# Loading four rows of w_down per partition at the very start of a decode block, with the unused matmuls of the tail laid out anew

## The chip, the cores and the metric

The kernel runs on one core of one Trainium2 chip. Its engines work side by side: TensorE (PE in the profile; PEld is its loading of weights), VectorE (DVE), ScalarE (ACT), GpSimd (POOL) and SyncE (SP). Here SP issues nearly all the transfers from the chip's memory; the transfers themselves run on 16 DMA engines. The metric is the time of one execution in microseconds (us). Lower is better. A profile shows one execution from the first to the last instruction, the span; the execution's own time is a little longer.

## The reference

One decode step of a transformer block for a single token: attention over a cache of 65,536 positions, then a gated feed-forward layer.

```
B, Sq, D = 1, 1, 1024;  Hq, Hkv, Sk, Dh = 32, 4, 65536, 128;  F = 3584      (bf16)

q = layernorm(x) @ wq                                  # 1024 x 4096
scores = q . k_cache * Dh**-0.5;  p = softmax(scores)  # 8 query heads share one k/v head
h = x + (p . v_cache) @ wo                             # 4096 x 1024
n = layernorm(h)
out = h + (gelu(n @ w_gate) * (n @ w_up)) @ w_down     # 1024 x 3584 twice, 3584 x 1024
```

Every weight and every cache entry is used once: 173 MB are read, nearly all of it the two caches.

## The kernel before, in words

The kernel is written by hand in program order. A small class, `Flow` (lines 17 to 105), records operations with the names of what each reads and writes, works out which waits between engines are needed, and `issue()` then sends them to the engines. Each engine does its own list in order and waits on semaphores. Everything from the first layer norm to the gated product is one such list, issued inside a section that the tile framework leaves alone (`tc.tile_critical`, line 587). At the start of a section SP executes a no-op that raises a semaphore, and the other engines wait for it; at its end SP waits for all engines. Line 95 is where `issue()` calls an operation, so most rows of the profile carry L95.

All transfers of weights and caches go through SP's one queue, in this order: w_q in two halves into slots 0 and 1 of a ring of four slots, then for each of 8 half-heads two K loads (slots 2 and 3) and one V load (slots 0 and 1), then wo, w_gate (7168 KB), w_up (7168 KB) and w_down. A load into a slot waits until the engines have finished with what was there. The small x goes through ACT's queue.

In the loop, DVE transposes K, PE makes the scores, ACT the exponentials, and PE multiplies by V. After the loop the attention output is normalised on DVE, and multiplied by wo. `ffn_in` (line 534) issues the load of w_gate or w_up, does 64 matmuls (eight input rows per partition, eight blocks each) and two DVE transposes. The product of gelu(gate) and up goes into `actz`, in columns padded with zeros so that a 32-wide window picks the row of the output that a matmul adds to.

w_down has 28 rows per partition, each 2 KB. The first 16 (`FA`) go to slot 0 in one load of 4096 KB, eight (`FB - FZ`) to slot 1 in one of 2048 KB, and the last four (`FZ`) to a buffer of their own, `w_end`, in two loads of three rows and one row (768 and 256 KB, line 592). The first of these two is issued at the end of the section, the second only once all engines have ended it. The output is summed in two banks of PSUM, `d_ps` and `d_odd`. The residual h is put there ahead, by eight small matmuls at line 568, while up's weights are on their way.

`down` (line 598) does one row of w_down: eight matmuls of 32 columns by 128, four of them side by side in the array. `parts` lists the two large loads with their semaphores. In a second section (line 610) PE waits for each in turn and does its rows; after that section it waits for the two loads of `w_end`. `stay_busy(n)` does n matmuls of 128 x 512 into a bank that nobody reads. Such matmuls compute nothing; in the kernel before there are four ahead of the wait for the 16 rows and four ahead of the wait for the eight. At the end DVE and ACT cast the two banks (lines 622 and 623) and SP sends the result out.

Of the kernel before, what the change touches and what calls it, by code (L numbers as in the profile page):

```python
# [11 lines left out]
BF16 = mybir.dt.bfloat16  # L12
# [4 lines left out]
class Flow:  # L17
# [13 lines left out]
    def op(self, e, call, r=(), w=(), after=(), wait=(), inc=None, dma=False, rows=None, **kw):  # L31
        i = len(self.ops)
        deps = {}

        def need(j, hard):
            o = self.ops[j]
            if o["e"] == e and not dma and not o["dma"] and (e == "pe" or not hard):
                return
            deps[j] = True

        for k in r:
            if k in self.writer:
                need(self.writer[k], True)
        for k in tuple(w) + tuple(after):
            if k in self.writer:
                need(self.writer[k], True)
            for j in self.readers.get(k, ()):
                need(j, False)
        if e == "pool":
            if self.rows[0] != rows and self.rows[1] is not None and not self.ops[self.rows[1]]["inc"]:  # L50
                deps[self.rows[1]] = True
            self.rows = rows, i
        last = {}
        for j in deps:
            o = self.ops[j]
            k = j if o["dma"] else o["e"]
            last[k] = max(last.get(k, j), j)
        deps = last.values()
        for k in r:
            self.readers.setdefault(k, []).append(i)  # L60
        for k in w:
            self.writer[k] = i
            self.readers[k] = []
        self.ops.append(dict(e=e, call=call, kw=kw, deps=sorted(deps), wait=wait, inc=inc, dma=dma))
# [44 lines left out]
def kernel(  # L109
# [13 lines left out]
    nc = tc.nc  # L123
    P = 128
    D = A_x.shape[-1]
# [4 lines left out]
    F = B_w_gate.shape[1]  # L130
    DC = D // P
# [14 lines left out]
    NB = 512  # L146
# [5 lines left out]
    eps = 1e-5  # L152
    assert Dh == P and rep * NS == SQ and NT % (CH * NH) == 0 and D % NB == 0 and F % NB == 0 and C4 == 4
    assert CPH == 4 and NH == 2

    FZ = 4
    w_end = nc.alloc_sbuf_tensor("w_end", [P, FZ, D], BF16)
# [3 lines left out]
    def sb(name, shape, dtype=F32):  # L161
        return const.tile(shape, dtype, name=name)
# [3 lines left out]
    qs = sb("qs", [P, 4, NS, P + 1], BF16)  # L166
    sc = sb("sc", [P, CPH, NN, rep, NS])
    pt = sb("pt", [P, CPH, NN, rep, NS], BF16)
    bank = [psum.tile([P, NB], F32, name="bank%d" % i) for i in range(8)]
    kt_bytes = ktb[:].rearrange("p c s w -> p (c s w)")  # L170

    def over(offset, shape, dtype=F32):

        n = 1
        for x in shape:
            n *= x
        if dtype == F32:
            v = kt_bytes[:, offset // 4:offset // 4 + n]
        else:
            v = kt_bytes[:, offset // 4:offset // 4 + n // 2].bitcast(BF16)  # L180
        if len(shape) == 2:
            v = v.rearrange("p (a b) -> p a b", a=shape[0])
        return v

    def slot(i, n=1):
        return ring[:, i * CW:(i + n) * CW]

    f = Flow(nc, tc)
    op = f.op
# [45 lines left out]
    def select(key, out, op_, fill, base, pattern, mult, rows=None):  # L235
# [14 lines left out]
       in_=ident_f[:].rearrange("p (q m) -> p q m", q=4).unsqueeze(2).to_broadcast([P, 4, NI, SQ]))  # L250
# [7 lines left out]
    sel16 = sb("sel16", [P, 16])  # L258
# [40 lines left out]
    def wide_rows(banks, bkeys, rows_z, zkey, ci, blocks, wkeys, first, last):  # L299

        for t, w in enumerate(blocks):
            q = t % 4
            op("pe", "matmul", r=[zkey] + wkeys, w=[bkeys[t // 4]], out=banks[t // 4][32 * q:32 * q + 32, :], lhsT=rows_z[:, ci, :], rhs=w,
               start=first, stop=last, tile_position=(0, 32 * q))

    def rows_to_columns(banks, bkeys, key, order="p n -> p n", **sizes):

        w = [ps.shape[-1] for ps in banks]
        r = over(28672, [sum(w)])
        o = 0  # L310
        for ps, n, bk in zip(banks, w, bkeys):
            src = ps.rearrange(order, **sizes)
            op("dve", "transpose", r=[bk], w=[key], out=r[:, o:o + n].rearrange("p (e j) -> p e j", j=32) if sizes else r[:, o:o + n], in_=src)
            o += n
        return r[:, 0:o:32]
# [10 lines left out]
    for q in range(4):  # L326
        op("pe", "matmul", r=["q_bf"] + ["esel"], w=["B5"], out=qsel_ps[:, :, q, :], lhsT=esel[:, q, :], rhs=q_bf[:],
           start=True, stop=True)
# [162 lines left out]
    for dq in range(OQ):  # L491
        op("pe", "matmul", r=["o_sb", "osel"], w=["B4"], out=o2_ps, lhsT=osel[:, dq, :], rhs=o_sb[:, dq * Hq:(dq + 1) * Hq],
           start=(dq == 0), stop=(dq == OQ - 1))
# [7 lines left out]

    FA = CW // D
    FB = FC - FA
    at_ps = bank[6][:]
    wv = slot(2, 2).rearrange("p (c n) -> p c n", c=Hq)
    f.dma("sp", wv, A_wo.rearrange("(p c) n -> p c n", p=P), w=["R2", "R3"], wait=done, sem=r_sem[2])
    for c in range(Hq):
        for s in range(DS):
            q = 2 * (c % 2) + s
            op("pe", "matmul", r=["o2z", "R2", "R3"], w=["B6"], out=at_ps[32 * q:32 * q + 32, :], lhsT=o2z[:, c, :],  # L510
               rhs=wv[:, c, :].rearrange("k (p s c) -> k s p c", s=DS, c=C4)[:, s], start=(c < 2), stop=(c >= Hq - 2), tile_position=(0, 32 * q))
# [12 lines left out]
    assert DC * F <= 2 * CW  # L524
    FW = [32 * FA, 32 * FB]

    def f_blocks(w_row):

        blocks = []
        for o, n in zip((0, P * FA), FW):  # L530
            blocks += [w_row[:, o + q * n:o + (q + 1) * n] for q in range(4)]
        return blocks

    def ffn_in(wmat, key, s0, b0):
        banks = [bank[b0 + i][:, 0:n] for i, n in enumerate(FW)]
        bkeys = ["B%d" % (b0 + i) for i in range(2)]
        rk = ["R%d" % s0, "R%d" % (s0 + 1)]
        wv = slot(s0, 2)[:, 0:DC * F].rearrange("p (c n) -> p c n", c=DC)
        f.dma("sp", wv, wmat.rearrange("(p c) n -> p c n", p=P), w=rk, sem=r_sem[s0], wait=[(s_step, STEPS * NT2 - 1)])
        for ci in range(DC):  # L540
            wide_rows(banks, bkeys, hz, "xz", ci, f_blocks(wv[:, ci, :]), rk, ci == 0, ci == DC - 1)
        return rows_to_columns(banks, bkeys, key, "p (j e) -> p e j", j=32)
# [15 lines left out]
    OB = D // OR  # L558
    orow = [30, 94, 31, 95, 32, 96, 33, 97]
    d_ps = bank[2][:, 0:OB]  # L560
    op("dve", "memset", w=["B2"], ap=d_ps, constant=0.0)
    hb = over(10240, [DC, P])
# [2 lines left out]
       in0=h_col[:].unsqueeze(2).unsqueeze(3).to_broadcast([P, DC, OR // 2, 2]),  # L565
       in1=o_of[:].rearrange("p (a b) -> p a b", b=2).unsqueeze(1).to_broadcast([P, DC, OR // 2, 2]), op=ALU.mult)
    for j in range(DC):
        op("pe", "matmul", r=["hb", "sel16"], w=["B2"], out=d_ps[:, j:OB:DC], lhsT=hb[:, j, :], rhs=sel16[:],
           start=False, stop=False, skip_group_check=True)
    d_odd = bank[7][:, 0:OB]  # L570
    op("dve", "tensor_copy", r=["B2"], w=["B7"], out=d_odd[64:P, :], in_=d_ps[64:P, :])
# [2 lines left out]
    actz = over(16384, [FC, 2 * AZ + 2], BF16)  # L574
    op("pool", "memset", w=["actz"], ap=actz, constant=0.0)
    u_r = ffn_in(B_w_up, "u_r", 2, 0)
    op("dve", "tensor_tensor", r=["u_r", "gl", "actz"], w=["actz"], out=actz[:, :, AZ], in0=u_r, in1=gl[:], op=ALU.mult)

    wa = slot(0)[:, 0:FA * D].rearrange("p (e n) -> p e n", e=FA)
    wb = slot(1)[:, 0:FB * D].rearrange("p (e n) -> p e n", e=FB)  # L580
    wb_src = B_w_down[P * FA:F, :].rearrange("(p e) n -> p e n", p=P)
    parts = [(wa, 0, FA, f.dma("sp", wa, B_w_down[0:P * FA, :].rearrange("(p e) n -> p e n", p=P), after=["R0"], inc=(r_sem[0], 16)), r_sem[0])]
    e0 = 0
    w_body = wb_src[:, e0:FB - FZ, :]
    part = wb[:, e0:FB - FZ, :]
    parts.append((part, FA + e0, FB - FZ - e0, f.dma("sp", part, w_body, after=["R1"], inc=(r_sem[1], 16)), r_sem[1]))
    with tc.tile_critical(no_gpsimd_drain=True):  # L587
        f.issue()

    ends = []  # L590
    for i, (e1, e2) in enumerate(((FB - FZ, FB - 1), (FB - 1, FB))):
        d = nc.sync.dma_start(out=w_end[:, e1 - FB + FZ:e2 - FB + FZ, :], in_=wb_src[:, e1:e2, :])
# [5 lines left out]
    def down(a_row, w_row, landed=None):  # L598
        for j in (0, 4, 1, 5, 2, 6, 3, 7):
            q, m = divmod(orow[j], 32)  # L600
            mm = nc.tensor.matmul((d_ps, d_odd)[q // 2][32 * q:32 * q + 32, :], lhsT=a_row[:, AZ - m:AZ - m + 32], rhs=w_row[:, j * OB:(j + 1) * OB],  # L601
                             start=False, stop=False, skip_group_check=True, tile_position=(0, 32 * q))
            if landed is not None:
                tc.declare_no_dep(mm.ins, landed.ins, query=mybir.DependencyQuery.ANY, reason="TensorE waits for the load's own semaphore ahead of it")

    def stay_busy(n):
        for i in range(n):
            nc.tensor.matmul(bank[5][:], lhsT=qs[:, 0, 0, 0:P], rhs=qs[:, 1 + i % 3].rearrange("p s c -> p (s c)")[:, 0:NB], start=True, stop=True)

    with tc.tile_critical(no_gpsimd_drain=True):  # L610
        for w_rows, a0, n, at, sem in parts:
            stay_busy({0: 4, FA: 4}.get(a0, 0))
            nc.tensor.wait_ge(sem, at)
            for e in range(n):
                down(actz[:, a0 + e, :], w_rows[:, e, :])
    with tc.manual_schedule(engines={mybir.EngineType.PE}):
        for i, (d, e1, e2) in enumerate(ends):
            nc.tensor.wait_ge(end_sem[i], 16)
            for e in range(e1, e2):
                down(actz[:, FA + e, :], w_end[:, e - FB + FZ, :], d)  # L620
# [34 lines left out]
```

## Time and profile before

| | |
|---|---|
| Median of 3 runs | 409.91 us (409.71 to 410.13) |
| Profiled execution | 409.64 us |
| its span | 407.8 us |
| PE busy | 229.4 us (56%) |
| DVE busy | 202.5 us (50%) |
| ACT busy | 39.5 us (10%) |
| POOL busy | 19.3 us (5%) |
| Read from memory | 173.02 MB, 424 GB/s over the span |
| Mean granted clock of TensorE | 0.807 of full speed |

The profiled execution's time is 1.8 us more than its span, which begins with the first instruction and ends with the last. Where the prediction speaks of a place, it means us from the start of the span. The granted clock is the share of TensorE's clock that the chip lets through; in this trace it is 0.5 or 1.0 at any one time. "L601 x32" is 32 instructions from line 601. In a timeline row the columns are start, length, engine, line, operation, output and input, shape and count, and in brackets the idle time ahead of it and what ended that; "issue" there means that the trace shows nothing that was waited for. In the view of transfers, q1 is SP's queue and q8 carries instructions.

### The profile page before, as it was taken

To read this page: it belongs to the slowest core of one execution; us is meant where nothing else is said; L and a number is where in the kernel's file an instruction comes from. 1 tells how busy PE (TensorE), PEld (TensorE's weight loads), DVE (VectorE), ACT (ScalarE), POOL (GpSimd) and SP (SyncE) were. 2 spreads that over 40 slices of the span, in tenths; PEclk is the share of its full clock that TensorE was granted. 3 is DMA by queue.
4 is the path that set the end of the run, shared out by engine and by line. 5 is a ranking of instruction groups with operands and counts; after the bars stand their busy time and mean duration, and the time that the engine had idled before them with its cause. 6 is when DMAs were issued, how large, how long until landed. Compare 5 with 4: busy or idle time off the path is not lost. (4 is left out here: it accounts for less than half of the span.)

```text
span 407.8 us, 3913 instructions
## 1 busy us (share of the span) xinstructions
PE 229.4 (56%) x1647; PEld 102.4 (25%) x1647; DVE 202.5 (50%) x174; ACT 39.5 (10%) x141; POOL 19.3 (5%) x39
## 2 busy tenths in 40 slices
PE   0431865584657467735874486468466737254166
PEld 0210322231322233212321232223132213132125
DVE  1216870885089428924980678088609931021110
ACT  1000003001200210030003000300130030000000
POOL 4210000001000000010000001000000000020000
PEclk9975896699669866988896889569968988586767
DMA  8999999999999999999998999999999999999995
GB/s 335 437 411 458 418 456 415 460 418 406 460 460 418 411 412 501 418 405 424 450 463 373 456 424 440 424 460 418 411 444 469 418 418 418 464 440 424 407 411 225
DMA packets 4815, 173.12 MB, mean 425 GB/s; under 512 B 580, under 2 KB 584, under 8 KB 840
## 3 DMA queue, kind: packets, MB, share of 16 engines
q1 hardware_dynamic: 4760, 173.02, 98.5%
q8 instruction: 5, 0.08, 0.1%
q14 instruction: 2, 0.02, 0.0%
q10 hardware_dynamic: 48, 0.00, 0.0%
HBM read 173.02 MB, written 0.00 MB: 424 GB/s over the span
## 5 line engine op out<-in xcount | busy, mean ns | idle before, releaser
L95 DVE STREAM_TRANSPOSE ktb<-ring 128x4096 f32<-128x4096 f32 x32 | 141.1, 4418 | 83.8 <-DMA ring<-in_A_k_cache_dram 83.8
L430 PE MATMUL bank<-ktb,qs 128*128 128x512 bf16 x512 | 131.4, 415 | 61.7 <-PEq L416 61.7
L430 PEld LDWEIGHTS bank<-ktb,qs 128*128 128x128 bf16 x512 | 51.2, 103 | 138.7 <-issue 92.5
L442 PE MATMUL bank<-ring,pt 128*32 128x512 bf16 x512 | 45.9, 537 | 36.5 <-PEq L416 36.5
L95 ACT ACTIVATE pt<-sc,nb 128x256 bf16<-128x256 f32 x64 | 31.5, 494 | 254.1 <-DVE nb L95 254.1
L442 PEld LDWEIGHTS bank<-ring,pt 128*32 128x32 bf16 x512 | 19.1, 129 | 60.1 <-issue 56.8
L95 DVE STREAM_TRANSPOSE sc<-bank 128x512 f32<-128x512 f32 x32 | 22.3, 696 | 23.4 <-PE bank L430 23.4
L95 PE MATMUL bank<-ring,xz 128*32 128x512 bf16 (+1 forms) x192 | 17.1, 534 | 20.9 <-DMA ring<-in_B_w_up_dram 7.3
L95 DVE STREAM_TRANSPOSE ktb<-bank 128x512 f32<-128x512 f32 (+1 forms) x6 | 4.0, 672 | 33.0 <-PE bank L95 32.7
L95 DVE TENSOR_REDUCE mx<-sc 128x8 f32<-128x1536 f32 (+1 forms) x16 | 19.5, 1220 | 0.5
L95 POOL COPY qs<-qsel 32x128 bf16<-32x128 bf16 x16 | 7.9, 491 | 232.0 <-PE bank L430 217.4
L95 PEld LDWEIGHTS bank<-ring,xz 128*32 128x32 bf16 x192 | 6.8, 131 | 29.6 <-issue 16.0
L95 ACT ACTIVATION_READ_ACCUMULATOR pt<-sc,nb 128x1 f32 x64 | 11.9, 187 | 0.0
L451 PE MATMUL bank<-sel,acc_sb 128*128 128x8 f32 x64 | 8.2, 255 | 6.2 <-PEq L416 6.2
L434 PE MATMUL bank<-ident_f,mx 128*8 128x128 f32 x8 | 2.2, 269 | 14.6 <-PEq L416 14.6
L451 PEld LDWEIGHTS bank<-sel,acc_sb 128*128 128x128 f32 x64 | 7.7, 191 | 10.0 <-issue 10.0
L95 PE MATMUL bank<-ring,ktb 128*32 128x512 bf16 x64 | 5.4, 504 | 7.8 <-DMA ring<-in_A_wo_dram 7.8
L95 ACT COPY acc_sb<-bank 128x512 f32<-128x512 f32 x8 | 4.7, 586 | 48.5 <-PE bank L442 48.5
L95 DVE TENSOR_TENSOR h_col<-bank,x_col 128x8 f32<-128x8 f32 x1 | 0.2, 167 | 15.6 <-PE bank L95 15.6
L95 POOL MEMSET ktb<- 128x1024 bf16 (+2 forms) x3 | 3.5, 1165 | 74.2 <-PE bank L430 74.2
L436 PE MATMUL bank<-diag,ones_f 8*128 8x8 f32 x16 | 3.3, 273 | 5.7 <-PEq L416 5.7
L95 PE MATMUL bank<-sel,ktb 128*128 128x16 f32 (+1 forms) x24 | 4.0, 300 | 3.5 <-DVE bank L95 2.7
(87 smaller groups left out, 60.0 us busy)
## 6 DMA issues: line engine op xcount, KB each, us to landing
ring<-in_A_k_cache_dram SPq DMA_DIRECT2D x16, 4096.0 KB, 24.7
ring<-in_A_wq_dram SPq DMA_DIRECT2D x2, 4096.0 KB, 16.8
ring<-in_B_w_gate_dram SPq DMA_DIRECT2D x1, 7168.0 KB, 28.7
ring<-in_B_w_up_dram SPq DMA_DIRECT2D x1, 7168.0 KB, 28.3
ring<-in_B_w_down_dram SPq DMA_DIRECT2D x1, 4096.0 KB, 21.5
ring<-in_B_w_down_dram SPq DMA_DIRECT2D x1, 2048.0 KB, 26.1
w_end<-in_B_w_down_dram SPq DMA_DIRECT2D x1, 768.0 KB, 27.2
w_end<-in_B_w_down_dram SPq DMA_DIRECT2D x1, 256.0 KB, 10.1
```

The costliest lines, as they stand in the source:

```text
L95: ins = getattr(self.eng[e], o["call"])(**o["kw"])
L430: m = nc.tensor.matmul(bank[c][:], lhsT=qs[:, jt].rearrange("p s c -> p (s c)")[:, s * P:(s + 1) * P], rhs=mv[:, :, J, :, u], start=(s == ...
L434: nc.tensor.transpose(out=mxT_ps, in_=mx1[:], identity=ident_f[:]).then_inc(s_step, 1)
L436: nc.tensor.matmul(bc_ps, lhsT=ones_f[0:rep, :], rhs=diag[:], start=True, stop=True).then_inc(s_step, 1)
L442: m = nc.tensor.matmul(acc[32 * q:32 * q + 32, :], lhsT=pt[:, c, n, :, :].rearrange("p h s -> p (h s)"), rhs=v_sb[:, c, :, n, :], start=(c ...
L451: m = nc.tensor.matmul(o_ps, lhsT=acc_sb[:, u * Dh:(u + 1) * Dh], rhs=sel[:, u:SQ:NS], start=(u == 0), stop=(u == NS - 1))
```

## The change

Four of the eight rows per partition of slot 1 move out of it into a buffer of their own, `w_first`. Their load, 1024 KB, is the first thing that SP issues, ahead of the section's opening no-op. The load into slot 1 shrinks to four rows. `w_first` is waited for at the residual's small matmuls. Its 32 matmuls are issued between the two sections.

Ten matmuls that nobody reads are put behind up's 64, inside the first section. Of those in the tail, two stand ahead of the wait for the 16 rows, three ahead of the wait for the slot 1 rows, two ahead of the wait for the first `w_end` load and none ahead of the second.

```diff
+    FD = 16
+    FE = 4
+    wb_src = B_w_down[P * FD:F, :].rearrange("(p e) n -> p e n", p=P)
+    w_first = nc.alloc_sbuf_tensor("w_first", [P, FE, D], BF16)
+    first = nc.sync.dma_start(out=w_first[:], in_=wb_src[:, 0:FE, :])
+    first_sem = tc.alloc_semaphore("first_landed")
+    first.then_inc(first_sem, 16)
+    tc.no_tile_sem_insts.add(first.ins.name)
+
     FZ = 4
...
     for j in range(DC):
-        op("pe", "matmul", r=["hb", "sel16"], w=["B2"], out=d_ps[:, j:OB:DC], lhsT=hb[:, j, :], rhs=sel16[:],
+        op("pe", "matmul", r=["hb", "sel16"], w=["B2"], wait=[(first_sem, 16)], out=d_ps[:, j:OB:DC], lhsT=hb[:, j, :], rhs=sel16[:],
            start=False, stop=False, skip_group_check=True)
...
     u_r = ffn_in(B_w_up, "u_r", 2, 0)
+    for i in range(10):
+        op("pe", "matmul", w=["B5"], out=bank[5][:], lhsT=qs[:, 0, 0, 0:P], rhs=qs[:, 1 + i % 3].rearrange("p s c -> p (s c)")[:, 0:NB], start=True, stop=True)
...
-    e0 = 0
+    e0 = FE
     w_body = wb_src[:, e0:FB - FZ, :]
...
+    for e in range(FE):
+        down(actz[:, FA + e, :], w_first[:, e, :], first)
     with tc.tile_critical(no_gpsimd_drain=True):
         for w_rows, a0, n, at, sem in parts:
-            stay_busy({0: 4, FA: 4}.get(a0, 0))
+            stay_busy({0: 2, FA + FE: 3}.get(a0, 0))
             nc.tensor.wait_ge(sem, at)
...
         for i, (d, e1, e2) in enumerate(ends):
+            stay_busy((2, 0)[i])
             nc.tensor.wait_ge(end_sem[i], 16)
```

## The prediction, made before the result was known

> **What bounds the kernel now.** I read the page first: transfers are busy in nearly every slice, and the chain that ended last is transfers almost alone.
>
> ```profile
> span 407.8 us, 3913 instructions
> ...
> DMA  8999999999999999999998999999999999999995
> ...
> q1 hardware_dynamic: 4760, 173.02, 98.5%
> q8 instruction: 5, 0.08, 0.1%
> ...
> DMA 14%; PE 3%; SPq 0%; issue 0%; ACT 0%
> ...
> ring<-in_B_w_down_dram SPq DMA_DIRECT2D x1, 2048.0 KB, 26.1
> w_end<-in_B_w_down_dram SPq DMA_DIRECT2D x1, 768.0 KB, 27.2
> ```
>
> In the chain of waits, in order of time, the end follows the w_end transfer that lands at 404.28 (376.42 + 26.1 = 402.5 is the landing of the piece before it). What comes behind is short.
>
> ```profile
> 376.98 0.07 issue
> 377.05 27.23 DMA w_end<-in_B_w_down_dram
> 404.28 0.15 issue
> 404.43 0.84 PE bank L601 x32
> 405.27 0.02 issue
> 405.29 0.26 ACT h L623
> ```
>
> So two things can move the time: when the stream of transfers starts, and whether PE is still ready when the last piece lands. The timeline of PE over the tail shows the second.
>
> ```profile
> 395.45 1.89 PE L608 MATMUL bank<-qs 128*128 128x512 bf16 x4 [2.59 <-PEq L610]
> 397.56 3.60 PE L601 MATMUL bank<-ring,ktb 128*32 128x128 bf16 x128 [0.21 <-DMA ring<-in_B_w_down_dram]
> 401.09 1.37 PE L608 MATMUL bank<-qs 128*128 128x512 bf16 x4
> 402.47 0.62 PE L601 MATMUL bank<-ring,ktb 128*32 128x128 bf16 x30
> 403.40 0.68 PE L601 MATMUL bank<-ring,ktb 128*32 128x128 bf16 x34 [0.31 <-issue]
> 404.43 0.79 PE L601 MATMUL bank<-w_end,ktb 128*32 128x128 bf16 x32 [0.35 <-DMA w_end<-in_B_w_down_dram]
> ```
>
> The fifth line is the one to stop at. Sixty-four matmuls on the same landed piece break after 30, and for half a microsecond (from 402.87, when the next was due, to 403.40) PE waits for nothing that the trace names. I take it for instructions not yet there. The q8 row counts five instruction transfers of 16 KB. Narrow windows of the transfer view put them at 32.1, 357.9, 377.0, 400.9 and 405.3. A matmul is two instructions (PE and PEld both count 1647). Going back 256 instructions from the break, over 30 matmuls, the four of L608 and the rest, gives the 35th of the 128 matmuls, started at 398.5; 256 further back lies in gate's matmuls (374.9 at the latest); the next in wo's (354.1). Each stands two to four microseconds before one of those transfers, and the break itself stands 1.9 before the last. So PE seems to ask for the next block of 256 when it enters a block. The block asked for at 397.7 to 398.5 (PE's queue may run ahead of its matmuls) came into use at 403.40, some 5 us later. Today this costs nothing: the matmuls behind it end just before w_end lands.
>
> **The change part by part.** The sum is made on the profiled execution: span 407.8, time 409.64, which is 0.27 under the median of 409.91; I add the difference found to the median.
>
> Start of the stream. The first w_q issue stands at 1.02, behind the section's no-op at 0.79 and a branch. The new load is issued where the no-op stood: 0.23 earlier. Bounds: 0 (if something else holds the first bytes) to 0.30 (SP leaves the start barrier at 0.72). I take -0.23. The 1024 KB keep the stream busy for 2.46 us (the 2048 KB piece took 4.9, from 397.5 to 402.5), longer than the 0.43 by which w_q's issue moves back (one issue on SP takes 0.39 to 0.42), so no hole follows. POOL, DVE, ACT and PE wait for that no-op and start 0.43 later. POOL's constants end at 6.2 and are needed at 9.5. x, which ACT issues, lands at 9.5 behind w_q's packets; were it 2.4 later, xz would be ready at 17.5 for 15.1, and the first 32 matmuls (3.6) would still end before the second half of w_q, which lands at 22.9 and then at 25.1. That cover would have to lose 4 us before it cost anything.
>
> From there all transfers are 2.46 - 0.23 = 2.23 later up to w_up. Every stretch of 10 us in the loop has a transfer share of 0.93 or more, a 4096 KB load lands 24.7 after its issue, and gate's is issued 11.8 before wo lands: compute shifts along and holds up no issue. Behind w_up, w_down is 1024 KB shorter, and the last landings come 0.23 earlier. Two pieces for one: 768 KB took 1.8 us, the same rate, so 0 to +0.1, taken +0.06. Transfers alone: -0.17.
>
> The new wait of the residual's matmuls is for a load that landed some 370 us before: 0. w_first's room in SBUF: 0.
>
> PE's tail. Up lands at 387.83, so now at 390.06. Its matmuls took 5.02, the clock rising at 391.56. Granted clock changes only at 3.41 us steps (391.56, 394.97, 401.80), wherever these fall. Alike rows at 0.5 throughout would take 6.0, at 1.0 from early on 4.4. Up ends between 394.5 and 396.1; I take 395.4.
>
> Ten unused matmuls: at the full clock L608's last two stand 0.216 apart, at half clock 0.43. The clock is up when gate's and up's matmuls end, so 2.16; with their drain 397.8. DVE, whose last step came 1.7 behind up's matmuls, is ready at 397.2, so PE is now what SP waits for. SP's second w_end issue, queued behind that, moves from 394.8 to about 398.0; its data is due at 404.7 and not late. PE's next matmuls wait for the same.
>
> w_first's 32 matmuls: 0.45 at the rate of w_end's row (14 ns, without the last one's 0.22), from 398.1. They stand outside the section, so its start comes behind them: 0.2 for the last result and 0.7 (394.75 to 395.45 before). Two unused: 0.43. At 400.0 PE is ready for the 16 rows, landed at 397.5 + 2.23 = 399.75: 0.25 late already. At 14 ns they would end at 401.8 (before, at half clock, 26.7 ns each: 400.9).
>
> Now the block. Between up and the 16 rows stood 15 instructions; now there are 96 (20 for the ten, 64 for w_first, 4 for the two, 8 of waits and branches). The break moves 81 back, from behind 30 matmuls of the second piece to behind 122 of the 16 rows; the entry before it falls on the end of w_first's matmuls, 398.5. That is up to 0.8 later than before. From entry to use took 4.9 to 5.7; some of it was queueing behind 16 KB packets, where 6 and 8 KB ones now run. Bounds for the use: 402.6 (up early, no queueing) to 404.3 (up late, as before). I take 403.5, nearest to the one such row there is. PE waits from 401.7 to 403.5, and behind it stand: 6 matmuls 0.08, three unused 0.65, 32 matmuls 0.44, end of section 0.44 (403.86 to about 404.30 before), two unused 0.43, 32 matmuls to the last start and result 0.63: 2.67. The cast on DVE starts at 406.2 for 405.25: +0.95, in which the -0.23 is contained. 409.91 + 0.95 = 410.86.
>
> The Trainium skill, "Runtime: NRT & Kernel Launch", section "Instruction fetch mechanics", states blocks of 256 instructions with the next fetched while the current one runs, and calls the cost of crossing a boundary mostly hidden. The trace agrees on the blocks and not, at 403.40, on the hiding; by that rule the block term is nothing and the first rival's 409.74 would be the sum.
>
> **The rivals.** First, not slower: the block costs nothing because it comes in time. The half microsecond may be something else, or the earlier entry may be enough. Then PE ends the 16 rows at 401.8, the second piece at 402.9, the section at 403.4, its two unused at 403.8, and waits for w_end at 404.07: transfers decide, 409.91 - 0.17 = 409.74. For it: the chain is transfers today, and no other break shows. Against it: 256 instructions fit every instruction transfer. It decides once the block is there by 402.5.
>
> Second, slower still: the clock. If up's matmuls miss two steps, the ten run partly at half clock (up to 4.3 for 2.16) and the 16 rows too (3.4 for 1.7). PE then ends 1.3 to 3 later, about 412.1. For it: the clock fell at 394.97 after a step with PE busy 1.30 of 3.41, and stayed down after one with 2.72. Against it: the ten stand right behind up, and keep that step full.
>
> Third, faster: after 403 the transfer share is 0.32, then 0.06, so most engines are done early and a few finish the last landings. Were these few caught up by the new split, up to 1.2 could go, to 408.7, with PE in time. Nothing in the change addresses it.
>
> **How the numbers follow.** Two tenths of a per cent, 0.82 us, is about what a measurement of this kernel tells from no change. PE late through the block: 0.66, from +0.1 to +1.8, two thirds of it above 0.82. In time: 0.23, all within. Clock: 0.07. Faster: 0.04. Slower 0.43 + 0.07 = 0.50, within 0.23 + 0.23 = 0.46, faster 0.04. The range takes in the first two cases and leaves most of the others out: 409.6 to 411.9; the likeliest alone is 410.0 to 411.7.
>
> **What would show it.** Right: the first transfer's issue at 0.8; up landed near 390.1; ten unused matmuls to about 397.6; an unexplained break after some 122 matmuls of the 16 rows, ending after 403; w_end's matmuls behind PE, not behind their transfer. Wrong: no break, or w_end's transfer still ahead of the last matmuls; a granted clock of 0.5 over the 16 rows points to the second rival. Most sensitive is when the block comes into use: each 0.1 us there is 0.1 at the end.

## The result and the profile after

The changed kernel is slower: 414.0 us median (411.79 to 414.15) against 409.9 us (409.65 to 410.13) for the kernel before on the same chip, a ratio of the means of 1.0084 with a 95% interval of 1.0058 to 1.0110. (The medians stand further apart, because four of the six executions lie near 414 and two near 411.8.) The forecast was 410.86 with a range up to 411.9. The direction and the place were right, the size was not.

The profiled execution of the changed kernel took 414.12 us. First its page: span, transfers in forty slices, the queues with data and with instructions, and the chain that ended last.

```profile
span 412.1 us, 3932 instructions
...
DMA  8999999998999899989998999999999999999991
...
q1 hardware_dynamic: 4904, 173.02, 97.5%
q8 instruction: 5, 0.08, 0.1%
...
PE 0%; ACT 0%; issue 0%
PE bank L619 0%; PE bank L612 0%; ACT h L637 0%
```

Transfers have gone from the chain that ended last; before they were nearly all of it. The last slice of the transfer row falls from 5 to 1: the engines that move data are idle there, while the kernel goes on for longer. What is the last to end now is seen in the timeline of PE over the tail (start, length, and in brackets the idle time ahead and what ended it).

```profile
390.13 5.70 PE L95 MATMUL bank<-ring,xz 128*32 128x512 bf16 x64 [5.00 <-DMA ring<-in_B_w_up_dram]
395.76 2.33 PE L95 MATMUL bank<-qs 128*128 128x512 bf16 x10
398.31 0.63 PE L612 MATMUL bank<-w_first,ktb 128*32 128x128 bf16 x32 [0.22 <-SPq L598]
399.79 0.60 PE L619 MATMUL bank<-qs 128*128 128x512 bf16 x2 [0.85 <-PEq L623]
400.33 1.91 PE L612 MATMUL bank<-ring,ktb 128*32 128x128 bf16 x122
405.18 0.29 PE L612 MATMUL bank<-ring,ktb 128*32 128x128 bf16 x6 [2.94 <-issue]
405.40 1.45 PE L619 MATMUL bank<-qs 128*128 128x512 bf16 x3
406.78 1.04 PE L612 MATMUL bank<-ring,ktb 128*32 128x128 bf16 x32
408.04 0.99 PE L619 MATMUL bank<-qs 128*128 128x512 bf16 x2 [0.21 <-PEq L623]
408.96 0.63 PE L612 MATMUL bank<-w_end,ktb 128*32 128x128 bf16 x32
```

The 16 rows' matmuls break after exactly 122 of 128, and for 2.94 us PE waits for nothing that the trace names, with all its data in SBUF. The last w_end transfer lands at 404.77, before PE goes on. The view of PE in stretches of one step of the granted clock (busy time and number of instructions, granted clock, share and rate of the transfers) shows the second half of the loss.

```profile
core 0: us, PE busy (x), PEclk, DMA share, GB/s
398.60:402.00 3.40, 2.55 (x150) 1.00 0.96 396
402.00:405.40 3.40, 0.46 (x24) 1.00 0.31 119
405.40:408.80 3.40, 3.19 (x43) 0.51 0.02 5
```

The step with the break in it holds only 0.46 us of PE's work, and the next step runs at half clock: three unused matmuls take 1.45 us and 32 of w_down 1.04. The cast on DVE starts at 409.62; before it was 405.25.

### The profile page after: what moved, and what is told of

Same layout as the page of the kernel before. It is cut to its first block, busy times and chain, and to the rows that moved or that the text cites. A ratio compares the mean times of both kernels' runs of the same rounds, so it can differ in the third digit from the quotient of the medians.

```text
span 412.1 us, 3932 instructions
## 1 busy us (share of the span) xinstructions
PE 234.8 (57%) x1656; PEld 104.5 (25%) x1656; DVE 202.6 (49%) x174; ACT 39.4 (10%) x141; POOL 19.2 (5%) x39
## 5 line engine op out<-in xcount | busy, mean ns | idle before, releaser
L95 PE MATMUL bank<-ring,xz 128*32 128x512 bf16 (+1 forms) x192 | 18.6, 571 | 20.0 <-DMA ring<-in_A_wq_dram 9.4
L95 PE MATMUL bank<-sel,ktb 128*128 128x16 f32 (+1 forms) x24 | 5.6, 373 | 3.5 <-issue 2.8
```

The source lines that it names most:

```text
L95: ins = getattr(self.eng[e], o["call"])(**o["kw"])
```

## The experiments

Two main theories stood at first. The block theory says that the loss is the late block of instructions, which the change has moved to a worse place, and what follows from it. The other says that PE comes late by the work which the change puts in front of the 16 rows: the ten unused matmuls, w_first's 32 and the section start behind them. Later runs ask what made the block later than forecast. Ratios are to the kernel before on the same chip, with 95% intervals.

**Moving the blocks and nothing else.** Tiny unused matmuls (128 x 8) are put ahead of wo's matmuls, some 35 us before the tail, where PE is idle. Each is two instructions and shifts all that follows in the instruction stream.

```diff
+    for i in range(45):
+        op("pe", "matmul", w=["B5"], out=bank[5][:, 0:8], lhsT=qs[:, 0, 0, 0:P], rhs=qs[:, 1, 0, 0:8], start=True, stop=True)
     for c in range(Hq):          # wo's matmuls
```

> The changed kernel with 45 tiny unused matmuls (128x8) ahead of wo's matmuls, in idle time of PE some 35 us before the tail. They add 90 instructions in front of the tail and no work in it, so the places where PE enters a new block of 256 move 90 instructions ahead: the entry that asks for the block goes from the end of w_first's matmuls (398.7) to up's 62nd matmul (393 to 395.5), and the first instruction that needs the block from behind the 122nd of the 16 rows' matmuls to their 78th (about 401.4). Block theory (the late block costs the time): entry plus 4.9 to 6.5 is 398 to 402, so the break at 402.0 to 405.2 is gone or under 0.6 us, PE is ready for w_end when it lands (404.0 to 404.8), and the time is 409.5 to 410.4. Rival, added work on PE (the ten, w_first, the section start behind them): nothing of that is taken away, so the time stays at 412 to 414. Rival, clock (the tail runs at half clock whatever the block does): 411 to 412.5 with no break.

Measured: 409.66 us, ratio 0.9998 (0.9988 to 1.0007). Its tail on the timeline:

```profile
397.64 0.63 PE L614 MATMUL bank<-w_first,ktb 128*32 128x128 bf16 x32 [0.22 <-SPq L600]
399.00 0.61 PE L621 MATMUL bank<-qs 128*128 128x512 bf16 x2 [0.73 <-PEq L625]
399.72 1.97 PE L614 MATMUL bank<-ring,ktb 128*32 128x128 bf16 x128
401.62 0.82 PE L621 MATMUL bank<-qs 128*128 128x512 bf16 x3
402.37 0.63 PE L614 MATMUL bank<-ring,ktb 128*32 128x128 bf16 x32
403.22 0.59 PE L621 MATMUL bank<-qs 128*128 128x512 bf16 x2 [0.21 <-PEq L625]
404.05 0.93 PE L614 MATMUL bank<-w_end,ktb 128*32 128x128 bf16 x32 [0.24 <-DMA w_end<-in_B_w_down_dram]
```

All of the added work is there, 90 instructions more besides, and the loss is gone: 128 matmuls without a break, and w_end's wait for their transfer again. Adding instructions in an idle place has taken some 4 us off the kernel. The added-work theory falls, and so does a clock that is low whatever the block does (411 to 412.5 without a break).

The opposite, the kernel before with 34 of them:

> The kernel before with 34 such tiny matmuls ahead of wo's matmuls: 68 more instructions in front of the tail, none in it, no load moved. The entry that asks for the block goes from the 35th to the first of the 16 rows' matmuls, where PE's queue may run 1 to 2 us ahead of 397.6, and the instruction that needs it from behind the 30th of the second piece's matmuls to the unused matmuls ahead of them (about 401). Block theory: an unexplained break ahead of the second piece, from about 401.1 to between 402 and 404, behind it 64 plus 32 plus 32 matmuls and the unused ones, so the time is 409.9 to 411.5. Rivals (added work, clock): nothing in the tail has changed, 409.7 to 410.1 and no break there.

Measured: 410.08 us, ratio 1.0009 (0.9997 to 1.0021).

```profile
397.58 2.74 PE L603 MATMUL bank<-ring,ktb 128*32 128x128 bf16 x128
402.40 1.65 PE L610 MATMUL bank<-qs 128*128 128x512 bf16 x4 [2.08 <-issue]
403.98 1.90 PE L603 MATMUL bank<-ring,ktb 128*32 128x128 bf16 x64
406.33 0.63 PE L603 MATMUL bank<-w_end,ktb 128*32 128x128 bf16 x32 [0.45 <-PEq L612]
```

The break has moved to the unused matmuls ahead of the second piece, where the count of instructions puts it, and grown from 0.31 to 2.08 us. This execution took 411.49, but the median is not clearly above before: the second piece lands at 402.2 in any case, so that most of the break lies beside that wait. The trace bears the place out; the time alone would not have told.

**Taking the unused matmuls away.**

```diff
-    for i in range(10):
-        op("pe", "matmul", w=["B5"], out=bank[5][:], lhsT=..., rhs=..., start=True, stop=True)
```

> The changed kernel without the ten unused matmuls behind up's (20 instructions fewer and 2.3 us less of PE's time between up and w_first). Added-work rival: the ten are what makes PE late, so 2.2 us come back and the time is 409.6 to 411. Block theory: the entry moves to the 5th of the 16 rows' matmuls and the instruction that needs the block to the 2nd matmul behind them; PE comes to the entry 1 to 2 us earlier, or no earlier if it waits for the 16 rows' landing at 399.75, so the break still ends at 403.5 to 405.5 and the time is 411 to 414. Clock: without the ten PE's step behind up is emptier and the 16 rows may run at 0.5.

Measured: 411.23 us, ratio 1.0030 (1.0019 to 1.0041), inside the line of the block theory (411 to 414) and 0.23 above that of the added work (409.6 to 411); so near to both, the time alone does not decide.

```profile
399.86 3.59 PE L610 MATMUL bank<-ring,ktb 128*32 128x128 bf16 x128 [1.17 <-DMA ring<-in_B_w_down_dram]
403.39 0.82 PE L617 MATMUL bank<-qs 128*128 128x512 bf16 x3
404.14 0.23 PE L610 MATMUL bank<-ring,ktb 128*32 128x128 bf16 x1
404.52 0.63 PE L610 MATMUL bank<-ring,ktb 128*32 128x128 bf16 x31 [0.15 <-issue]
```

The break stands where counted, in the second piece, but it is short, because PE gets there late: the 16 rows' matmuls run at half clock, 3.59 us for 1.9. So leaving the ten out saves their 2.3 us and lets the clock fall, and the 16 rows then cost 1.6 us more. The kernel before, with the ten added, agrees from the other side: there the same 128 matmuls take 1.97 us for 3.60 (below).

With the tail's other unused matmuls left out as well (`stay_busy` at lines 625 and 631 gone):

> The changed kernel without any unused matmul behind up's: none of the ten, and none between the waits for w_down (34 instructions fewer). Added-work rival: all of PE's extra work but w_first's 32 matmuls is gone, so 409.6 to 410.5. Block theory: the entry falls on the 7th of the 16 rows' matmuls (landed at 399.75), the need on the 7th matmul of the second piece, so a break still stands ahead of or in the second piece, ending at 403.5 to 406, and with PE at half clock behind it the time is 411 to 414.5.

Measured: 414.90 us, ratio 1.0125 (1.0109 to 1.0142). A miss for both:

```profile
398.14 0.63 PE L610 MATMUL bank<-w_first,ktb 128*32 128x128 bf16 x32 [1.87 <-SPq L596]
404.96 4.53 PE L610 MATMUL bank<-ring,ktb 128*32 128x128 bf16 x160 [6.19 <-PEq L621]
```

PE waits 6.19 us at the section start, and the trace has the reason: one instruction there waits for two semaphores from 398.27 on, the section's and a second one, and lasts until just behind the landing of w_end's first load at 404.21. With nothing on PE between the section and w_end's matmuls, the tile framework's scheduler had put that wait together with the section's own, ahead of the 16 rows. The run says nothing on the block. With the two unused matmuls ahead of w_end's wait put back (line 631 as in the changed kernel):

> The run without any unused matmul, with the two that stand ahead of w_end's wait put back. If that run's 414.9 came from the wait for w_end's first load being drawn ahead of the section start (PE stood there until 404.2, the landing of that load), the wait is back in its place, the 16 rows' matmuls start at 399.8 to 400.1, at half clock, the break is small (need at the second piece's 5th matmul), and the time is 410.6 to 411.8. If it came from the missing unused matmuls themselves (clock, block): 413 to 415.

Measured: 411.15 us, ratio 1.0029 (1.0015 to 1.0043), as expected for a wait back in its place. In the profiled execution the 16 rows' matmuls start at 399.93, and the break stands behind the fourth matmul of the second piece, where it was counted; at 2.08 us it is not the small one that was expected.

**One part alone.** The ten unused matmuls put into the kernel before:

> The kernel before with the ten unused matmuls behind up's and nothing else of the change. Block theory: the entry is the 25th instead of the 35th of the 16 rows' matmuls and the break stands behind 20 instead of 30 matmuls of the second piece, ending at 402.6 to 403.6 with 44 instead of 34 matmuls behind it: 409.6 to 410.4. Added-work rival (the ten make PE late by themselves): they end at 395.3, with the section start and the four unused behind them the 16 rows' matmuls start at 398.3 or later for 397.56 and all that follows moves back by 0.7 to 2: 410.4 to 412.

Measured: 410.22 us, ratio 1.0009 (0.9996 to 1.0023).

```profile
397.56 1.97 PE L603 MATMUL bank<-ring,ktb 128*32 128x128 bf16 x128 [0.57 <-DMA ring<-in_B_w_down_dram]
402.48 0.46 PE L603 MATMUL bank<-ring,ktb 128*32 128x128 bf16 x20 [1.98 <-DMA ring<-in_B_w_down_dram]
403.73 0.80 PE L603 MATMUL bank<-ring,ktb 128*32 128x128 bf16 x44 [0.79 <-issue]
```

The ten cost nothing that can be told; the break moves from behind 30 to behind 20 matmuls, as counted, and ends 0.13 later than the latest that was expected (403.6). What the ten are worth once the block is out of the way (the changed kernel without them, 55 tiny ones ahead of wo's so that the blocks lie as in the first run):

> The changed kernel without the ten unused matmuls, and with 55 tiny ones ahead of wo's matmuls, so that the block is asked for at up's 62nd matmul and needed at the 16 rows' 78th, as in the run with 45. What the ten are worth once the block is out of the way. If they only hold the clock up: the 16 rows' matmuls run at half clock as in the run without the ten (3.59 us for 1.6 to 2.0), PE is ready for w_end about 1 us after it has landed, and the time is 410.3 to 411.0. If they are only added work: 409.5 to 409.9.

Measured: 410.61 us, ratio 1.0016 (1.0006 to 1.0026), for 0.9998 with the ten. The difference, 0.0018 of 410, is some 0.7 us, between two intervals that just touch. The profiled execution happened to be the lowest of its kernel (409.51, the others 410.26 to 411.33) and ran the 16 rows at full clock, so that the cause of the difference is argued from the run without the ten, not shown here.

**Why the block came so late.** Narrow windows of the view of transfers list the 16 KB packet with the instructions where it starts. For the changed kernel from 402.70 to 402.75, then for the kernel before from 400.9 to 401.0:

```profile
q8 instruction: 1, 0.02, 135.8%
```

```profile
q8 instruction: 1, 0.02, 67.1%
```

By the trace's records the packet started at 402.72, 4.0 us behind the execution of the first matmul of the block before it (398.7; this is called the entry from here on); in the kernel before it was 2.5 (398.5 to 400.96). From the packet's start to the use of its instructions it is 2.2 to 2.6 us in the fourteen traces that show such a break. So the question is what lies ahead of the packet. One theory says that it waits behind the data in the transfer queues (queue theory), the other that PE asks for it late (late-request theory). Two shifts that move the entry within w_first's matmuls, by 22 and by 10 tiny ones:

> The changed kernel with 22 tiny unused matmuls (44 instructions) ahead of wo's matmuls, to tell why the block's packet started 4.0 to 4.3 us behind the entry. The entry moves from w_first's last matmul to its 10th, which PE's queue reaches at the same time (398.4), and the need from the 122nd to the 100th matmul of the 16 rows. Queue theory (the packet waits behind the many small data packets of the queue, some 4 us whatever PE does): packet at 402.4 to 402.8, break until 404.9 to 405.3, time 411.8 to 414.2. Late-request theory (PE asks only when it is 12 to 27 instructions into the block, which in the changed kernel is behind the section start and the wait for the 16 rows, at 399.8 to 400.3): here those instructions are w_first's, so the packet starts at 400.4 to 401.6, the break ends at 402.9 to 404.1, and the time is 409.9 to 411.8.

> The same with 10 tiny matmuls (20 instructions): the entry at w_first's 22nd matmul, the need behind the 112th of the 16 rows' matmuls. Queue theory: packet at 402.4 to 402.8, time 411.8 to 414.2. Late-request theory: the place 12 to 27 instructions on lies between w_first's 28th matmul and the end of the section start, so the packet comes 0.3 to 2.3 earlier than 402.7 by where in these 15 instructions the request stands: 400.4 to 402.4, time 410 to 413.5.

> The changed kernel itself once more, for a second trace of the block's packet and beside the same runs of before as the two shifts: 411.8 to 414.2, a break behind the 122nd of the 16 rows' matmuls. Queue theory: the packet's start may wander by a microsecond from run to run, since the queue does. Late-request theory: it stands 2.0 to 3.0 behind the first of the 16 rows' matmuls, as in the first trace (2.4).

Measured: 412.80 us, ratio 1.0073 (1.0045 to 1.0101); 413.93 us, 1.0077 (1.0056 to 1.0098); and 413.80 us, 1.0083 (1.0054 to 1.0111). Each break stands where counted, behind 100, 112 and 122 matmuls. Packets started at 401.12, 402.48 and 402.59, for entries at 397.6, 398.8 and 399.75. Neither theory got all three. The late request hit the packet and the break of the first, though not its time (411.8 at most), missed the second narrowly (402.4 and 413.5 us at most), and missed the third (1.24 us behind the first of the 16 rows' matmuls, for 2.0 to 3.0 expected). The queue hit all three times and missed the packet of the first (402.4 at the earliest). What all three share is 2.8 to 3.7 us between entry and packet.

One guess was that the branch at the section start, just behind the entry, held the request back. In the next kernel w_first's matmuls stand inside the second section, behind its start (their load becomes the first operation of the first section's list):

```diff
-    for e in range(FE):
-        down(actz[:, FA + e, :], w_first[:, e, :], first)
     with tc.tile_critical(no_gpsimd_drain=True):
+        for e in range(FE):
+            down(actz[:, FA + e, :], w_first[:, e, :])
```

> The changed kernel with w_first's matmuls inside the second section, behind its start, instead of ahead of it (its load is issued as first of the first section). The section start's waits and branch then stand 57 instructions ahead of the entry (w_first's 29th matmul) instead of 2 to 8 behind it; the need stays at the 16 rows' 123rd matmul. Branch theory (a branch close behind the entry holds the request back: packets started 1.10 to 1.13 behind the entry in seven places without a branch near and idle queues, 1.83 to 2.54 in three places with one within 68 instructions): the request goes out with the entry, 398.9 to 399.7, the packet starts 1.7 to 2.5 later, 400.8 to 402.1, the break ends at 403.2 to 404.5, time 410 to 412. Queue theory (the packet waits 3 to 4.3 behind the entry in this stretch): packet 402.3 to 403.6, break until 404.7 to 406, time 412 to 414.5.

Measured: 414.21 us, ratio 1.0101 (1.0085 to 1.0118).

```profile
399.32 0.63 PE L610 MATMUL bank<-w_first,ktb 128*32 128x128 bf16 x32 [0.87 <-PEq L619]
399.88 0.61 PE L617 MATMUL bank<-qs 128*128 128x512 bf16 x2
400.42 1.91 PE L610 MATMUL bank<-ring,ktb 128*32 128x128 bf16 x122
405.40 0.29 PE L610 MATMUL bank<-ring,ktb 128*32 128x128 bf16 x6 [3.07 <-issue]
```

Entry at 399.7, 57 instructions behind the branch (w_first's matmuls begin at 399.3), packet at 403.05: 3.3 us, inside the queue theory's line and outside the other. The branch guess falls. The Trainium skill, "Runtime: NRT & Kernel Launch", section "Instruction fetch mechanics", warns that a taken branch to a place outside the two loaded blocks forces a fetch. No run here tests that sentence; this one only shows that the delay is there too when no branch stands close behind the entry.

The same with 45 tiny matmuls ahead of wo's, as a version that might beat both:

> The same with 45 tiny matmuls ahead of wo's, so that the block is asked for in up's matmuls (as in the run that undid the loss): a version that may beat both. Block theory: no break, w_end's matmuls behind their transfer, 409.4 to 410.0, at best some 0.2 below the kernel before, which a measurement hardly tells. If the section start's place mattered by itself, 410.3 or more.

Measured: 409.88 us, ratio 0.9993 (0.9983 to 1.0003): without the break again, and not told apart from the kernel before.

Then the queue itself. PE's instructions stay as they are in the changed kernel, and data are taken away that would stand behind the 16 rows:

```diff
-    f.dma("sp", part, w_body, ...)
+    f.dma("sp", part[:, :, 0:32], w_body[:, :, 0:32], ...)          # first run only
...
-        d = nc.sync.dma_start(out=w_end[:, ..., :], in_=wb_src[:, e1:e2, :])
+        d = nc.sync.dma_start(out=w_end[:, ..., 0:32], in_=wb_src[:, e1:e2, 0:32])
...
-                down(actz[:, FA + e, :], w_end[:, e - FB + FZ, :], d)
+                down(actz[:, FA + e, :], w_first[:, e - FB + FZ, :], first)
```

> The changed kernel with PE's instructions unchanged, but of the second piece and of both w_end loads only the first 64 bytes of each row are loaded, so that 2 MB less stand in the queue behind the 16 rows; w_end's matmuls read w_first in its place. The output's last eight rows of w_down are wrong by that, and the time is that of a kernel with less to load. Queue theory (the block's packet waits behind data): entry at 398.4 to 399.5, packet 1.1 behind it as with idle queues, or at the landing of the 16 rows at the latest, 399.5 to 400.7, use 402.0 to 403.2, break at most 1 us. Late-request theory (PE asks late): the packet still starts 3 to 4 behind the entry, 401.5 to 403, and the break is 2 us or more.

> The same with the second piece loaded in full and only the two w_end loads cut to 64 bytes a row (1 MB less in the queue). Queue theory: the packet starts between that of the run before and that of the changed kernel, 400.0 to 402.2, no later than the end of the second piece on its engine. Late-request theory: 401.5 to 403, as there.

Measured: 409.40 us, ratio 0.9986 (0.9975 to 0.9998), and 410.24 us, 1.0012 (1.0001 to 1.0024). PE at the break, in the run with all of it cut and then in the run with half of it cut:

```profile
399.97 1.91 PE L612 MATMUL bank<-ring,ktb 128*32 128x128 bf16 x122 [0.51 <-DMA ring<-in_B_w_down_dram]
402.06 0.29 PE L612 MATMUL bank<-ring,ktb 128*32 128x128 bf16 x6 [0.18 <-issue]
```

```profile
400.13 1.91 PE L612 MATMUL bank<-ring,ktb 128*32 128x128 bf16 x122
402.62 0.29 PE L612 MATMUL bank<-ring,ktb 128*32 128x128 bf16 x6 [0.58 <-issue]
```

In the first of the two the break is all but gone, in the second it is down to 0.58 us, and the packets start at 399.84 and 400.19, for 402.72 and 402.59 in the changed kernel's two traces. To see how much of that is scatter, a third trace of the changed kernel and a second with half the queue:

> The changed kernel, a third trace. Queue theory: the block's packet starts at 402.3 to 403.1, near the end of the data on its engine, 2.6 to 4.2 behind the entry. If the spread is chance that has nothing to do with the data: anywhere from 1.5 to 4.3 behind the entry, so possibly at 400 to 401.5.

> The run with the two w_end loads cut to 64 bytes a row (the output is wrong by that), a second trace. Queue theory: the packet starts at 400.0 to 402.2, no later than the end of the second piece on its engine, and earlier than in the third trace of the changed kernel. If it is chance: up to 403.

Measured: 410.75 and 410.13 us, one execution each. With half the queue the packet started at 400.24, once more early, 2.0 us behind the entry (1.55 in the first trace). The changed kernel's third trace was a surprise:

```profile
389.92 4.86 PE L95 MATMUL bank<-ring,xz 128*32 128x512 bf16 x64 [7.43 <-DMA ring<-in_B_w_up_dram]
399.65 1.91 PE L612 MATMUL bank<-ring,ktb 128*32 128x128 bf16 x122 [0.41 <-DMA ring<-in_B_w_down_dram]
403.30 0.29 PE L612 MATMUL bank<-ring,ktb 128*32 128x128 bf16 x6 [1.75 <-issue]
403.75 0.59 PE L619 MATMUL bank<-qs 128*128 128x512 bf16 x2 [0.16 <-issue]
405.64 0.63 PE L612 MATMUL bank<-w_end,ktb 128*32 128x128 bf16 x32
```

```profile
core 0: us, PE busy (x), PEclk, DMA share, GB/s
396.70:400.10 3.40, 2.03 (x68) 1.00 0.80 334
400.10:403.50 3.40, 1.65 (x112) 1.00 0.80 321
403.50:406.90 3.40, 2.40 (x74) 1.00 0.06 19
```

Here the clock rose early in up's matmuls (4.86 us for 5.70), the entry came at 397.7 for 398.7, the packet at 400.85 (3.15 behind it; the expected line of the queue theory, 402.3 to 403.1, is missed), use at 403.30 for 405.18, and the break fell so across the clock's steps that none of them was nearly empty: the tail ran at full clock. The same program took 414.12 there and 410.75 here. (It ran on another chip than the first two, but the kernel with w_first inside the section took 414.2 on that one.) Of the 3.3 us between the two casts (409.62 and 406.31), 1.88 are the earlier use of the block and 1.4 the tail behind it (4.44 and 3.01 us), so the clock's share of the loss is some 1.4 us between these two traces. The step ahead of the fall is not always nearly empty: in the second trace (413.56 us) one with 1.60 us of PE's work was followed by half clock, and here one with 1.65 was not, so no limit can be read from these runs. The executions of the changed kernel lie near 411.8 and near 414 besides this one; for 411.8 there is no trace.

What the queue runs settle: with PE's instructions the same and less data behind the 16 rows, the packet starts 1.55 to 2.05 us behind the entry in three traces, for 2.8 to 4.0 in the three traces of the changed kernel. With all the data it took 2.0 to 4.0 in the eight traces that have w_first's load and enter the block in w_first's or the 16 rows' matmuls. What stays open is which packets it waits for, and whether that is all: the same loads gave 2.0 in one run (entry at 399.9, without the ten) and 4.0 in another (398.7), and the run with 2 MB less took 2.04, longer than the 1.55 with 1 MB less.

## Why the prediction was right or wrong

- **Start of the stream: right.** First issue at 0.805, first packets at 1.83 for 2.04, up landed at 390.08 (forecast 390.06), the last transfer at 404.77 for 404.87, which is 0.10 earlier where 0.17 was forecast. The whole gain that the change could bring is of this size, and the two kernels without the break (0.9998 and 0.9993) do not show it beyond doubt.
- **The chain of PE up to the 16 rows: right.** Up's matmuls ended at 395.8 (395.4), the ten at 398.1 (397.8), w_first's began at 398.3 (398.1), the 16 rows' at 400.33 (400.0), and ran at full clock. SP's second w_end issue at 398.33 did no harm.
- **The place of the break: right.** Behind 122 matmuls, to the instruction, and, in every later trace that shows a break, where the count put it. The Trainium skill, "Runtime: NRT & Kernel Launch", section "Instruction fetch mechanics", calls the cost of crossing into the next block mostly hidden; the 2.94 us here and the loss undone by 45 tiny matmuls decide against it for this tail.
- **When the block comes into use: wrong, +1.68.** The step that failed is "I take 403.5, nearest to the one such row there is", and its bound of 404.3: it was 405.18. From entry to use 6.5 us went by, where 4.9 to 5.7 had been read from a single row. The reason given for the lower part, that 6 and 8 KB packets stand ahead now instead of 16 KB ones, brought nothing that shows: the packet started 4.0 us behind the entry instead of 2.5, and 2.8 to 4.0 in the three traces of this kernel. One row cannot give the spread of such a wait.
- **What stands behind the block: wrong, +1.77.** The sum of 2.67 us took the full clock for it. It took 4.44 (405.18 to 409.62), 3.19 of it in one step at a clock of 0.51. The forecast had such a fall in its own rows (the clock fell after a step with 1.30 us of PE in 3.41) and used it for a rival, but not on the break that it forecast itself: the break left 0.46 us of PE's work in its step. Together 403.5 + 2.67 + 1.68 + 1.77 = 409.62, the start of the cast (the forecast's 406.2 is 406.17, rounded). The Trainium skill, "TensorE: Matmul & The Clock Gate", section "Part 1: The HAM clock gate (the "warmup" mystery)", says that the window of some 3.4 us runs on its own and does not start with the kernel; the 3.4 us steps and the two traces at 414.12 and 410.75 agree.
- **The rivals.** "The block comes in time" was worth 409.74; with the block moved, 409.66 was measured, so its price fits, and its condition was not met. The clock rival's 412.1 put the half clock at the ten and the 16 rows, which ran at full clock; the half clock came behind the break. The third, caught-up stragglers, did not show: the last landings were 0.10 earlier, no more, and by the trace's semaphore records the sixteen parts of the last load still land over 1.8 us (403.09 to 404.87 before, 402.94 to 404.77 after).
- **The range.** Its top, 411.9, came from the late end of the block at full clock. The two errors are not independent, since the later block causes the empty step; the range had to be carried through that. The third trace shows the case that was forecast: use at 403.30 (403.5) and a tail of 3.01 us at full clock (2.67) gave 410.75 us for 410.86. That is one of twelve executions; the others took 411.7 to 414.33.

## What to carry to other kernels

Count TensorE's instructions where the tail is tight: the boundaries of 256 lie at fixed places in the stream, a block is asked for only one block ahead, and in the eight traces named above, with transfers running, it came into use 4.6 to 6.5 us after the entry. An edit that adds or removes a few matmuls moves the boundary, and its effect on the time may be that and not its own work; a run with some tiny matmuls in an idle place tells the two apart. A forecast of a gap on TensorE must go on to ask what the gap does to the clock behind it.

## What the runs showed of the hardware that was not expected

- In the fourteen traces with a break, the 16 KB instruction packet took 0.95 to 1.10 us on its transfer engine, and PE went on 2.2 to 2.6 us behind its start (402.72 to 405.18 in the changed kernel). With at most some 0.3 MB of data still to be moved (the block after the one spoken of) it started 1.10 to 1.13 us behind the entry in eleven traces, for instance 405.18 to 406.28 and 405.40 to 406.51; with all the data queued behind the 16 rows, 2.0 to 4.0 in the eight.
- In the kernel before (403.40 to 405.34) and in three others the same wait was 1.8 to 2.5 us; in all four a section's end stands at most 34 matmuls behind the entry, and in the eleven it stands further off. That is a coincidence seen afterwards, not tested.
- One program, one input, and 410.75 to 414.33 us in twelve executions: a block that comes into use at 403.30 or at 405.18, and clock steps of 3.4 us that fall differently across the gap, spread a kernel by nearly one per cent. The kernel before spread by 0.5 us beside the first six of them (409.65 to 410.13) and by 1.6 us over all its executions (409.58 to 411.19).
